# State attention and hard-swish FFN on one core: two pairs of w_out and the second batch's tokens are staged in the output tiles, and the order of the opening is written anew

## The chip, the cores and the metric

The kernel runs on one core of one Trainium2 chip. The metric is the device time of one execution in microseconds (us). A run of a kernel gives one such time; three runs of the kernel before gave 656.95, 657.22 and 658.18 us, median 657.22. A further execution was recorded by the hardware profiler; all times of single instructions come from it. The engines are TensorE (PE, with its weight loads shown apart as PEld), VectorE (DVE), ScalarE (ACT), GpSimd (POOL) and SyncE (SP), whose queue (SPq) issues almost all transfers. Each engine works through its own queue in order.

## The reference

Attention between tokens `x` (8 batches, 8 heads, 512 tokens, 64 columns) and a small state (32 rows per head), in both directions, and then a feed-forward layer over all 4352 result rows:

```python
scores  = scale * x @ state.T            # per batch and head: 512 x 32
a       = softmax(scores)                # over the 32 state rows
xread   = a @ state                      # 512 x 64
scores2 = scale * state @ x.T            # 32 x 512
sread   = softmax(scores2) @ x           # 32 x 64
y = concat([xread, sread], axis=2)       # 544 rows per batch, 8 heads x 64 = 512 columns
h = y @ w_in                             # 512 -> 2048
out = (h * clip(h + 3, 0, 6) / 6) @ w_out  # 2048 -> 512
```

Inputs and output are float32. (The reference draws `x` and the weights at random; 512 of the 544 rows of each batch are tokens, 32 are state rows.)

## The kernel before

**Work on PE.** The tokens' result is never formed: since `xread @ w_in` is `a @ (state @ w_in)`, the kernel forms, for each batch, W' = state x w_in ("wp", by `wprime`, matmuls at line 507) and then h = a x W' (`first`, line 977 for the first step of the first batch and 948 elsewhere). A *step* is one block of 128 columns of h: there are 16 per batch and 16 more for all batches' state rows. `first(n)` forms the block into a PSUM bank `ps_h`; ACT and DVE make g of it (lines 998 and 1000: a relu of h + 3 and then min and product) and split g into a high and a low part (`split`, lines 305 and 306, `g_hi` and `g_lo`); `second(n)` multiplies these with 128 rows of w_out into four accumulators `acc0` to `acc3`, three matmuls of 512 columns each (high x high, high x low, low x high). Step 0 of the first batch is done plainly, in full float32 (line 977 for its first product, 1017 for its second).

**Weights.** Each w_in and w_out piece is loaded in 16-bit halves by SP (`weight`, line 370) into a staging tile, and put together by ACT (line 379, into one of two `tops` tiles) and DVE (line 384, the "join"). w_in pieces are joined into their home `w_in0` to `w_in3`. w_out pieces are joined in place and then split into `w_out_hi` (ACT, line 410) and `w_out_lo` (DVE, line 412). Staging tiles are three `raw` tiles (512 KB each) and four `early` tiles, which are the later homes of w_out's last chunks; the table `PLACES` says which piece lies in which. A piece can only be loaded once the tile's earlier content has been used up.

**Attention.** For each batch the tokens are turned (`take_in`): the first batch on PE (line 617), later ones by transfers in blocks of 32 x 32 (`load_turned`, line 494, sixteen transfers into two `raw` tiles) and four stream transposes on DVE (line 607). Then come the scores by columns (`scores_by_columns`, line 507 with `tmp` and `stT`, or 520 for the first batch), the softmax on DVE and ACT, and the exponentials for the other direction, which are turned by a transpose on DVE into blocks (line 871, in a `raw` tile) and sixteen transfers (`weights_moved`, line 879, into another `raw` tile). The first batch's weights of the softmax are made in an output tile `ot` (key `bt`) by `tokens_by_rows`, turned by PE (line 713), and copied back (lines 715 and 716).

**Output tiles.** The pool `outp` has two tiles of 1 MB, tag `ot`. They hold the first batch's softmax, every third W' from the second batch on, and the finished rows of a batch before they are stored (line 1052).

**What sets the order.** The whole program is a plan: `T`, `V`, `S_` and `Q` add an operation of PE, DVE, ACT and SP's queue with an estimated cost, a rank, what it reads and writes and the buffers it takes; `Plan.order` puts all operations in one row, and each engine's queue is that row's operations of its engine. The table `OPENING` fixes the beginning of the row by operation numbers (631 of them); from there the planner takes, on each engine, the ready operation of the lowest rank by its estimated times. `issue` writes the instructions in that order, and up to the first product puts filler matmuls (`wake`) where the planner thinks that PE would stand idle.

Of the kernel before, what the change touches and what calls it, by code (L numbers as in the profile page):

```python
# [10 lines left out]
F32 = mybir.dt.float32  # L11
# [55 lines left out]
class Plan:  # L67
# [33 lines left out]
    def order(self):  # L101
# [22 lines left out]
        while len(row) < n_ops:  # L124
# [44 lines left out]
            if size:  # L169
                channel = max(channel, t + 0.5) + size / self.transfer  # L170
                done = max(channel, t) + 2.0
                flying.remove(min(flying))
                flying.append(done)
# [33 lines left out]
def tile_state_attention_then_hardswish_ffn(  # L207
# [8 lines left out]
    nc = tc.nc  # L216
# [73 lines left out]
    def Q(rank, size, do, reads=(), writes=(), after=()):  # L290
        return plan.add("Q", 0.49, rank, do, reads, writes, after, size)
# [974 lines left out]
```

## Time and profile before

| | |
|---|---|
| median of three runs | 657.22 us (656.95 to 658.18) |
| profiled execution | 655.46 us |
| its span, first to last instruction | 653.7 us |
| granted clock of PE, mean | 0.999 |
| PE busy | 641.6 us, 3934 matmuls |
| DVE busy | 393.0 us |
| ACT busy | 293.1 us |
| transfers | 46.25 MB in 135270 packets |

How to read the views: a *window* row gives the busy time of each engine in a stretch, the granted clock of PE, the busy share of the 16 DMA engines and what they moved. A *timeline* row gives start, duration, engine, line, operation, the tile written and the tiles read (numbers left out), partitions x elements, count, and in brackets how long the engine stood idle before it and what it waited for. The matmuls are pipelined: one that shows 0.39 us lies half over the next, so the distance of two starts says what one costs. A wait inside a group that was begun shows as a longer matmul, not as idle time. The *chain of waits* is the work that ended last, followed back from the end. SPq rows are the queue's own time for issuing; a row that covers several transfers includes the waits between them.

### The profile page before, as it was taken

The page shows a single profiled execution, that of the slowest core. Times are in us where ns is not written, and L with a number is a line of the kernel's source. Part 1 is how long each engine was busy: PE and PEld are TensorE (multiplying, and loading weights), DVE is VectorE, ACT ScalarE, POOL GpSimd, SP SyncE. Part 2 cuts the span into 40 slices and gives each one's busy share as a digit, 9 for nine tenths or more (in the row PEclk, how much of TensorE's full clock was granted, in tenths as well). Part 3 has the DMA queues.
Part 4 walks back from the last instruction along what each step waited for, and adds up shares of the span by engine and source line. Part 5 has one row for each costly group of instructions (what it writes and reads, how often), then busy time and mean ns, then how long its engine had stood idle before and what let it go on. Part 6 is the DMA issues. An engine that isn't in the chain of part 4 may idle for free.

```text
span 653.7 us, 9891 instructions
## 1 busy us (share of the span) xinstructions
PE 641.6 (98%) x3934; PEld 500.3 (77%) x3934; DVE 393.0 (60%) x685; ACT 293.1 (45%) x510; POOL 1.2 (0%) x7
## 2 busy tenths in 40 slices
PE   8999999989999999999999999999999999999997
PEld 6577778767877877787868777787778787788896
DVE  6988785468487356944686356834595344443552
ACT  5988454334344343633344344534344333433542
POOL 0000000000000000000000000000000000000000
PEclk9999999999999999999999999999999999999999
DMA  8985500604840503132131405041131001000101
GB/s 285 339 268 179 117 10 10 118 15 107 120 133 11 86 2 103 33 51 46 64 70 20 78 1 134 1 76 21 66 66 30 3 1 66 0 1 2 64 1 33
DMA packets 135270, 46.25 MB, mean 71 GB/s; under 512 B 123576, under 2 KB 129208, under 8 KB 135096
## 3 DMA queue, kind: packets, MB, share of 16 engines
q1 hardware_dynamic: 135080, 45.36, 28.5%
q8 instruction: 31, 0.51, 0.3%
q10 hardware_dynamic: 144, 0.26, 0.1%
q14 instruction: 15, 0.12, 0.1%
HBM read 33.02 MB, written 8.91 MB: 64 GB/s over the span
## 4 chain that ended last, share of the span: by engine, by line
PE 85%; SPq 4%; DMA 4%; DVE 3%; ACT 2%; issue 1%; DVEq 0%; ACTq 0%
PE acc L948 51%; PE ps_h L948 27%; PE ps_s L507 4%; PE ps_h L507 2%; SPq L879 1%; SPq L494 1%; DMA raw<-in_x_dram 1%; DMA early<-in_moe_w_out_dram 1%; PE ps_h L905 1%; SPq L478 1%; ACT tops L379 1%; DMA early<-in_moe_w_in_dram 1%; DMA raw<-raw 1%; DVE w_in L384 0%; ACT g L998 0%
## 5 line engine op out<-in xcount | busy, mean ns | idle before, releaser
L948 PE MATMUL acc<-w_out_hi,g_hi 128*128 128x512 f32 x540 | 213.4, 395 | 0.1
L948 PE MATMUL acc<-w_out_lo,g_hi 128*128 128x512 f32 x540 | 210.6, 390 | 0.0
L948 PE MATMUL acc<-w_out_hi,g_lo 128*128 128x512 f32 x540 | 210.2, 389 | 0.0
L998 ACT ACTIVATE g<-ps_h,three 128x512 f32<-128x512 f32 (+1 forms) x144 | 95.6, 664 | 221.9 <-PE ps_h L948 210.9
L1000 DVE SCALAR_TENSOR_TENSOR g<-g,ps_h 128x512 f32<-128x512 f32 (+1 forms) x144 | 94.3, 657 | 150.7 <-ACT g L998 149.9
L948 PEld LDWEIGHTS acc<-w_out_hi,g_hi 128*128 128x128 f32 x540 | 101.4, 188 | 34.5 <-issue 12.6
L306 DVE TENSOR_TENSOR g_lo<-g,g_hi 128x512 fp32r<-128x512 f32 (+1 forms) x143 | 93.9, 657 | 49.2 <-ACT g_hi L305 48.0
L305 ACT CAST g_hi<-g 128x512 fp32r<-128x512 f32 (+1 forms) x143 | 85.0, 595 | 85.1 <-DVE g L1000 80.3
L948 PEld LDWEIGHTS acc<-w_out_hi,g_lo 128*128 128x128 f32 x540 | 101.4, 188 | 21.7 <-DVE g_lo L306 0.2
L948 PEld LDWEIGHTS acc<-w_out_lo,g_hi 128*128 128x128 f32 x540 | 101.5, 188 | 19.6
L948 PE MATMUL ps_h<-aT_hi,wp_hi 128*128 128x512 f32 (+1 forms) x246 | 90.4, 367 | 3.3 <-DVE wp_lo L306 2.9
L948 PE MATMUL ps_h<-aT_hi,wp_lo 128*128 128x512 f32 (+1 forms) x246 | 89.1, 362 | 0.4 <-DVE wp_lo L306 0.4
L948 PE MATMUL ps_h<-aT_lo,wp_hi 128*128 128x512 f32 (+1 forms) x246 | 89.1, 362 | 0.0
L948 PEld LDWEIGHTS ps_h<-aT_hi,wp_hi 128*128 128x128 f32 x246 | 46.4, 189 | 13.4 <-issue 3.6
L948 PEld LDWEIGHTS ps_h<-aT_lo,wp_hi 128*128 128x128 f32 x246 | 46.4, 189 | 8.2 <-DVE aT_lo L306 0.5
L948 PEld LDWEIGHTS ps_h<-aT_hi,wp_lo 128*128 128x128 f32 x246 | 46.4, 189 | 7.8 <-DVE wp_lo L306 0.7
L948 PE MATMUL ps_h<-aT_hi,wp 128*128 128x512 f32 x144 | 50.2, 389 | 0.0
L948 PEld LDWEIGHTS ps_h<-aT_hi,wp 128*128 128x128 f32 x144 | 27.0, 188 | 5.7
L607 DVE STREAM_TRANSPOSE tmp<-raw 128x512 f32<-128x512 f32 x28 | 19.1, 699 | 15.9 <-DMA raw<-in_x_dram 12.3
L948 PE MATMUL ps_h<-aT_lo,wp 128*128 128x512 f32 x72 | 28.0, 389 | 0.0
L379 ACT CAST tops<-early 128x512 f16<-128x512 bf16 x25 | 18.2, 779 | 5.0 <-DMA early<-in_moe_w_out_dram 2.8
L507 PE MATMUL ps_s<-w_in,stT 64*32 64x512 f32 (+1 forms) x320 | 19.6, 548 | 0.0
(124 smaller groups left out, 427.4 us busy)
## 6 DMA issues: line engine op xcount, KB each, us to landing
xb<-in_x_dram SPq DMA_DIRECT2D x32, 256.0 KB, 4.2
out_dram<-ot SPq DMA_DIRECT2D x8, 1024.0 KB, 4.4
raw<-in_x_dram SPq DMA_DIRECT2D x112, 64.0 KB, 2.1
early<-in_moe_w_in_dram SPq DMA_DIRECT2D x7, 1023.0 KB, 5.8
early<-in_moe_w_out_dram SPq DMA_DIRECT2D x4, 1023.5 KB, 5.4
raw<-raw SPq DMA_DIRECT2D x112, 32.0 KB, 2.0
raw<-in_moe_w_out_dram SPq DMA_DIRECT2D x7, 511.8 KB, 7.1
early<-in_moe_w_in_dram SPq DMA_DIRECT2D x2, 511.0 KB, 6.4
```

Of the source, the lines that this page charges most:

```text
L305: S_(cost, rank, lambda: nc.scalar.copy(hi(), src()), reads, [writes[0]])
L306: V(cost, rank, lambda: nc.vector.tensor_tensor(lo(), src(), hi().bitcast(F32), op=ALU.subtract), [*reads, writes[0]], [writes[1]])
L379: nc.scalar.copy(out[..., 1], digits(pieces().bitcast(BF16), 2, i))
L478: nc.sync.dma_start(x_tile(b)[:, :, k, :], x_v[b, k])
L494: nc.sync.dma_start(t[rows, i].rearrange("t (a c) -> t a c", c=NS), x[b, 4 * g + 2 * i + u, :, k * NS : (k + 1) * NS].rearrange("(a t) c - ...
L507: nc.tensor.matmul(out[u][cols, :], made["stT", b][rows, cols], moving(q)[rows], start=True, stop=True,)
L607: V(0.7, rank[0], lambda q=q, key=key: nc.vector.transpose(xT(b, q), made[key][:, q % 2]), [(*key, q % 2, u, k) for u in range(2) for k in ...
L879: nc.sync.dma_start(dst[:, :, q], src[:, :, c])
L905: nc.tensor.matmul(bank(pr)[cols, u * D : (u + 1) * D], e2T(b, u)[:, j * P + q * NS : j * P + (q + 1) * NS], x_tile(b)[:, NG * q + u, j, : ...
L948: nc.tensor.matmul(ps, l, r, start=start and k == 0, stop=stop and k == n - 1)
L998: S_(cost + 0.05, rank, lambda: nc.scalar.activation(g(), bank(ps)[:, :width], AF.Relu, bias=three), [ps], [g_key])
L1000: V(cost, rank, lambda: nc.vector.scalar_tensor_tensor(g(), g(), 6.0, bank(ps)[:, :width], op0=ALU.min, op1=ALU.mult), [ps], [g_key])
```

## The change

Three things change.

1. In `PLACES`, the w_out pairs 4-5 and 6-7 no longer go to `early2` and `early3` but to output tiles (`("ot", ("w", 0))` and `("ot", ("w", 1))`, named `wide`), and their loads wait for the subtractions of the first softmax (`first_exps`). `early2` and `early3` so first hold w_in pair 8 and pair 10 (and w_out 3 before that in `early3`).
2. The second batch's turned tokens (`load_turned` and `take_in` for b = 1) go to an output tile instead of two `raw` tiles; for later batches they stay in `raw`.
3. `OPENING` is written anew, 670 numbers, and the planner's estimates of costs and of transfers are altered (a queue operation 0.53 for 0.49, 0.62 for a turned-token load, 0.65 for a move; the transfer's landing is counted from its share of the channel). These estimates enter the program only through the order.

```diff
 OPENING = """
-5 2 1 0 24 3 4 35 11 80 36 27 6 29 30 28 93 31 32 33 14 49 34 41 25 19 50 51 37 26 52 42 38 39 53 43 57 54 44
+5 0 1 2 11 3 4 33 24 80 34 27 93 28 31 29 6 30 32 35 19 41 36 12 14 49 42 43 160 37 13 44 39 38 45 50 40 46
...
             if size:
-                channel = max(channel, t + 0.5) + size / self.transfer
-                done = max(channel, t) + 2.0
+                channel = max(channel, t + 1.3) + size / self.transfer
+                done = channel + 1.6
...
+            if place[0] == "ot":
+                return get(place, lambda: outp.tile([P, 2, 512, 2], U32, name="wide", tag="ot"))
...
-        Q(load_rank, {("in", 1): 537.0, ("in", 2): 925.0, ("out", 1): 465.0, ("out", 2): 930.0}[kind, n], load, writes=[key])
+        Q(load_rank, {("in", 1): 537.0, ("in", 2): 960.0, ("out", 1): 465.0, ("out", 2): 1000.0}[kind, n], load, writes=[key],
+          after=first_exps if place[0] == 'ot' else ())
...
+    def turned_tile(key):
+        if key[0] == "raw":
+            return get(key, lambda: stage.tile([P, 2, S], F32, name="raw"))
+        return get(key, lambda: outp.tile([P, J, DO], F32, name="ot"))[:, 2 * key[2] : 2 * key[2] + 2]
...
-            key = ("raw", ("x", b, g))
+            key = ("raw", ("x", b, g)) if b > 1 else ("ot", ("x", b), g)
...
-                            t = get(key, lambda: stage.tile([P, 2, S], F32, name="raw"))
+                            t = turned_tile(key)
...
-                key = ("raw", ("x", b, q // 2))
+                key = ("raw", ("x", b, q // 2)) if b > 1 else ("ot", ("x", b), q // 2)
                 V(0.7, rank[0], lambda q=q, key=key: nc.vector.transpose(
-                    xT(b, q), made[key][:, q % 2]),
+                    xT(b, q), turned_tile(key)[:, q % 2]),
...
-            V(0.35, r[1], lambda m1=m1, view=view, bt=bt: nc.vector.tensor_tensor(
+            shifted = V(0.35, r[1], lambda m1=m1, view=view, bt=bt: nc.vector.tensor_tensor(
                 bt(), view(), wide(m1()), op=ALU.subtract), [m1_key, ps], [part_key])
+            first_exps.append(shifted)
...
-        ("in", 4): ("early0", 1), ("in", 6): ("early1", 1), ("out", 4): ("early2", 1),
-        ("out", 6): ("early3", 1), ("in", 8): ("early2", 2), ("in", 10): ("early3", 2),
+        ("in", 4): ("early0", 1), ("in", 6): ("early1", 1), ("out", 4): ("ot", ("w", 0)),
+        ("out", 6): ("ot", ("w", 1)), ("in", 8): ("early2", 2), ("in", 10): ("early3", 2),
```

What this does to the queues is seen in three places. Lines of the changed kernel are 3 to 11 higher.

**DVE at the end of the opening.** The rows run from the end of the first softmax to the g of step 0 (1000, now 1011). `w_in_314` and `w_in_308` hold the softmax's turned weights, `nm` the maxima for the other direction, `wp_lo` and `aT_lo` the low parts of W' and of the weights, and rows that end in `tops` are joins. Before:

```order
L781 TENSOR_REDUCE nm_297<-ps_s 128x2
L384 SCALAR_TENSOR_TENSOR w_in_179<-early_142,tops 128x4x128 x2
L716 COPY w_in_314<-acc_308 128x512
L781 TENSOR_REDUCE nm_297<-ps_s 128x2
L306 TENSOR_TENSOR wp_lo<-acc_253,wp_hi 128x128
L784 TENSOR_TENSOR nm_297<-nm_297 128x2
L306 TENSOR_TENSOR aT_lo<-w_in_314,aT_hi 128x512
L787 TENSOR_SCALAR nm_297<-nm_297 128x2
L306 TENSOR_TENSOR aT_lo<-w_in_314,aT_hi 128x512
L306 TENSOR_TENSOR wp_lo<-acc_252,wp_hi 128x128
L384 SCALAR_TENSOR_TENSOR early_168<-early_168,tops 128x512
L1000 SCALAR_TENSOR_TENSOR g<-g,ps_h 128x512
```

and of the change:

```order
L716 TENSOR_TENSOR ot<-ot,s_190 128x8x32 x2
L387 SCALAR_TENSOR_TENSOR w_in_216<-early_137,tops 128x4x128 x2
L307 TENSOR_TENSOR wp_lo<-acc_264,wp_hi 128x128
L727 COPY w_in_308<-acc_302 128x512
L307 TENSOR_TENSOR wp_lo<-acc_265,wp_hi 128x128
L387 SCALAR_TENSOR_TENSOR raw<-raw,tops 128x512
L307 TENSOR_TENSOR aT_lo<-w_in_308,aT_hi 128x512 x2
L792 TENSOR_REDUCE nm_337<-ps_s 128x2 x2
L1011 SCALAR_TENSOR_TENSOR g<-g,ps_h 128x512
L795 TENSOR_TENSOR nm_337<-nm_337 128x2
L798 TENSOR_SCALAR nm_337<-nm_337 128x2
L416 TENSOR_TENSOR w_out_lo_362<-raw,w_out_hi_214 128x512
```

The maxima `nm` have moved from between the joins and copies to a place behind `aT_lo`, and the join of w_out piece 3 (`early_168`, now `early_155`) has moved from before the g of step 0 to behind it.

**SP after the first weights.** The rows begin with the w_out pair 4-5, in `early_444` or `wide`; w_in pairs 4-5 and 6-7 stand ahead of them in both. `wide` are the two w_out pairs, `ot<-in_x_dram` and `raw<-in_x_dram` the turned tokens, `st_raw` the next batch's state. Before:

```order
L370 DMA early_444<-in_moe_w_out_dram 128x2x2047
L370 DMA raw<-in_moe_w_out_dram 128x2047
L370 DMA early_497<-in_moe_w_out_dram 128x2x2047
L440 DMA st_raw<-in_state_dram 32x4x32 x4
L370 DMA raw<-in_moe_w_out_dram 128x2047
L370 DMA early_562<-in_moe_w_in_dram 128x4x1023
L370 DMA early_595<-in_moe_w_in_dram 128x4x1023
L370 DMA early_641<-in_moe_w_out_dram 128x2x2047
L370 DMA early_683<-in_moe_w_out_dram 128x2x2047
L494 DMA raw<-in_x_dram 32x16x32 x16
```

and of the change:

```order
L373 DMA wide<-in_moe_w_out_dram 128x2x2047
L445 DMA st_raw<-in_state_dram 32x4x32 x4
L373 DMA wide<-in_moe_w_out_dram 128x2x2047
L373 DMA early_461<-in_moe_w_in_dram 128x4x1023
L373 DMA early_475<-in_moe_w_in_dram 128x4x1023
L373 DMA raw<-in_moe_w_out_dram 128x2047 x2
L504 DMA ot<-in_x_dram 32x16x32 x6
L373 DMA early_599<-in_moe_w_out_dram 128x2x2047
L504 DMA ot<-in_x_dram 32x16x32
L373 DMA early_612<-in_moe_w_in_dram 128x4x1023
L504 DMA ot<-in_x_dram 32x16x32
```

The two w_out pairs stand directly behind w_in pair 6-7 now (before, two w_in pairs and a single piece lay between), and the turned tokens of the second batch are spread around the pair of w_out 8-9 (`early_599`) and the last pair of w_in (`early_612`) instead of standing behind all pairs.

**DVE at the third batch's tokens.** The rows are the stream transposes of the third batch (607, now 617) with what stands around them. Before:

```order
L1000 SCALAR_TENSOR_TENSOR g<-g,ps_h 128x512
L306 TENSOR_TENSOR g_lo<-g,g_hi 128x512
L607 STREAM_TRANSPOSE tmp<-raw 128x512 x2
L306 TENSOR_TENSOR g_lo<-g,g_hi 128x512
L306 TENSOR_TENSOR wp_lo<-ps_s,wp_hi 128x512
L306 TENSOR_TENSOR wp_lo<-ps_h,wp_hi 128x512
L1000 SCALAR_TENSOR_TENSOR g<-g,ps_h 128x512
L306 TENSOR_TENSOR g_lo<-g,g_hi 128x512
L306 TENSOR_TENSOR wp_lo<-ps_s,wp_hi 128x512
L1000 SCALAR_TENSOR_TENSOR g<-g,ps_h 128x512
L607 STREAM_TRANSPOSE tmp<-raw 128x512 x2
L306 TENSOR_TENSOR wp_lo<-ps_h,wp_hi 128x512
```

and of the change:

```order
L456 STREAM_TRANSPOSE stT<-st_raw 128x128
L1011 SCALAR_TENSOR_TENSOR g<-g,ps_h 128x512
L307 TENSOR_TENSOR wp_lo<-ps_h,wp_hi 128x512
L617 STREAM_TRANSPOSE tmp<-raw 128x512
L307 TENSOR_TENSOR wp_lo<-ps_s,wp_hi 128x512
L307 TENSOR_TENSOR wp_lo<-ps_h,wp_hi 128x512
L307 TENSOR_TENSOR g_lo<-g,g_hi 128x512 x2
L307 TENSOR_TENSOR wp_lo<-ps_s,wp_hi 128x512
L617 STREAM_TRANSPOSE tmp<-raw 128x512
L1011 SCALAR_TENSOR_TENSOR g<-g,ps_h 128x512
L824 RECIPROCAL r_831<-r_831 128x2
L617 STREAM_TRANSPOSE tmp<-raw 128x512 x2
```

Before, all four `wp_lo` stood behind the first two transposes and the last of them behind all four; now the first stands ahead of all transposes, the other three between the first and the second, and the last two transposes have no `wp_lo` behind them.

More of the change, by code (lines that the diff above doesn't have):

```diff
@@ L288, in S_, with Q @@
         return plan.add("S", cost, rank, do, reads, writes, after)
-    def Q(rank, size, do, reads=(), writes=(), after=()):
-        return plan.add("Q", 0.49, rank, do, reads, writes, after, size)
+    def Q(rank, size, do, reads=(), writes=(), after=(), cost=0.53):
+        return plan.add("Q", cost, rank, do, reads, writes, after, size)
     def get(key, make):
@@ L392, in weight @@
             top = ("top", (kind, k + i))
-            S_(0.62, rank, lambda i=i: upper(i), [key], [top])
+            S_(0.65, rank, lambda i=i: upper(i), [key], [top])
             V(0.62, rank, lambda i=i: join(i), [key, top],
@@ L425, in tile_state_attention_then_hardswish_ffn @@
     wp_at, scores_at = {}, {}
+    first_exps = []
     def load_state(b, rank, after=()):
@@ L443, in load_state @@
         if b < TURNED:
-            plan.add("Q", 1.35, rank, load, (), [key], after, 400.0)
+            plan.add("Q", 1.39, rank, load, (), [key], after, 400.0)
             return
-        plan.add("Q", 1.8, rank, load_blocks, (), [key], after, 400.0)
+        plan.add("Q", 2.6, rank, load_blocks, (), [key], after, 400.0)
     def turn_state(b, rank, after):
@@ L499, in load @@
                             )
-                        Q(rank, 65.536, load, writes=[(*key, i, u, k)], after=after)
+                        Q(rank, 65.536, load, writes=[(*key, i, u, k)], after=after, cost=0.62)
     def all_heads(b, out, moving):
@@ L795, in exps @@
                                              accum_out=r2()[:, NG + NG * i + u : NG + NG * i + u + 1])
-                    S_(0.6, rank(5), exps, [ps[i], n_key], [("tmp", ("e2", b, u), i), (*r_key, u, i)])
+                    S_(0.48, rank(5), exps, [ps[i], n_key], [("tmp", ("e2", b, u), i), (*r_key, u, i)])
             V(0.08, rank(6), lambda: nc.vector.scalar_tensor_tensor(
@@ L865, in move @@
                             nc.sync.dma_start(dst[:, :, q], src[:, :, c])
-                        Q(rank, 16.384, move, [blocks_key], [e2T_key(b, g, c, q)])
+                        Q(rank, 16.384, move, [blocks_key], [e2T_key(b, g, c, q)], cost=0.65)
             return
@@ L879, in move @@
                     nc.sync.dma_start(dst[:, :, q], src[:, :, c])
-                Q(rank, 32.768, move, [(*blocks_key, g) for g in range(NG)], [e2T_key(b, 0, c, q)])
+                Q(rank, 32.768, move, [(*blocks_key, g) for g in range(NG)], [e2T_key(b, 0, c, q)], cost=0.65)
     def put(c, ps, cols):
```

45 rows, old and new, of the table OPENING are left out of this document.

## The prediction

> **What bounds the kernel now.** I read the page first, then the waits of PE, then the windows, then PE's timeline where a window showed a gap.
>
> ```profile
> span 653.7 us, 9891 instructions
> PE 641.6 (98%) x3934; PEld 500.3 (77%) x3934; DVE 393.0 (60%) x685; ACT 293.1 (45%) x510; POOL 1.2 (0%) x7
> PE 85%; SPq 4%; DMA 4%; DVE 3%; ACT 2%; issue 1%; DVEq 0%; ACTq 0%
> ```
>
> PE is busy for 98% of the span, so an edit can only win where PE idles, fills or waits inside an instruction. The windows say where that is:
>
> ```profile
> 10.00:20.00 10.00, 8.80 (x119) 6.57 (x119) 9.93 (x31) 8.99 (x19) 0.00 (x0) 1.00 1.04 390
> 20.00:30.00 10.00, 9.63 (x56) 4.26 (x54) 9.85 (x22) 9.41 (x23) 0.00 (x0) 1.00 0.94 324
> 40.00:50.00 10.00, 9.60 (x59) 7.08 (x58) 8.37 (x13) 9.01 (x16) 0.00 (x0) 1.00 0.77 238
> 130.00:140.00 10.00, 7.08 (x103) 4.80 (x101) 4.65 (x8) 2.62 (x4) 0.00 (x0) 1.00 0.19 32
> 200.00:250.00 50.00, 50.00 (x245) 40.05 (x245) 26.95 (x43) 19.96 (x33) 0.00 (x0) 1.00 0.20 32
> ```
>
> The columns are the window, its length, then PE, PEld, DVE and ACT busy. From 10 to 30 us DVE works 19.8 of 20 us: the opening is DVE's. At 130 to 140 PE loses 2.9 us with DVE half idle. After 200 us nothing is lost, and there the order of the work is the same in both kernels. So all that can change lies in the first 140 us:
>
> ```profile
> 23.57 2.07 PE L1017 MATMUL acc<-raw,g 128*128 128x512 f32 x4
> ...
> 44.03 0.39 PE L948 MATMUL acc<-w_out_hi,g_lo 128*128 128x512 f32 x1
> 44.82 0.50 PE L948 MATMUL ps_h<-aT_hi,wp_hi 128*128 128x512 f32 x1 [0.40 <-DVE g L1000]
> ...
> 54.52 0.40 PE L948 MATMUL ps_h<-aT_hi,wp_lo 128*128 128x512 f32 x1
> 54.95 0.51 PE L948 MATMUL ps_h<-aT_hi,wp_hi 128*128 128x512 f32 x1
> ...
> 76.16 2.12 PE L507 MATMUL ps_s<-tmp,stT 64*32 64x512 f32 x16
> ...
> 132.13 0.39 PE L948 MATMUL acc<-w_out_lo,g_hi 128*128 128x512 f32 x1
> 132.35 0.39 PE L948 MATMUL acc<-w_out_hi,g_lo 128*128 128x512 f32 x1
> 135.66 0.47 PE L948 MATMUL ps_h<-aT_hi,wp_hi 128*128 128x512 f32 x1 [2.92 <-DVE wp_lo L306]
> ...
> 138.01 1.09 PE L507 MATMUL ps_s<-tmp,stT 64*32 64x512 f32 x16
> ```
>
> Two 512-wide matmuls start 0.2275 us apart on average (132.13 and 132.35 are two); read the others against that. 44.03 to 44.82 is 0.56 too long, 54.52 to 54.95 is 0.20 too long. The scores of the second batch take 2.12 us at 76.16, the same sixteen of the third 1.09 at 138.01: 1.03 us of waiting that the profile books as busy. Then the plain gap of 2.92. Together 4.71 us.
>
> **The change part by part.** Both kernels have 687 instructions on DVE, 495 on ACT and 318 on SP in the order; PE has seven fillers, each a weight load and a matmul, fewer, 36 for 43. No work is removed: it is a matter of what stands before what.
>
> *Opening.* What ends it is the g of step 0, which releases the first product with w_out at 23.57:
>
> ```profile
> 22.83 0.68 DVE L1000 SCALAR_TENSOR_TENSOR g<-g,ps_h 128x512 f32<-128x512 f32 x1
> 23.43 0.68 DVE L384 SCALAR_TENSOR_TENSOR raw<-raw,tops 128x512 uint32<-128x512 uint32 x1
> 24.03 1.28 DVE L412 TENSOR_TENSOR w_out_lo<-raw,w_out_hi 128x512 fp32r<-128x512 f32 x2
> ...
> 32.22 0.74 DVE L306 TENSOR_TENSOR wp_lo<-ps_s,wp_hi 128x256 fp32r<-128x256 f32 x2
> ...
> 61.29 2.52 DVE L412 TENSOR_TENSOR w_out_lo<-early,w_out_hi 128x1024 fp32r<-128x1024 f32 x2
> ```
>
> A 512-wide operation costs DVE 0.60 us from start to start (22.83, 23.43, 24.03), a half-wide one 0.37, a double one 1.26. Ahead of this g stand seven joins of weights before and six now, and two operations on two columns fewer (about 0.07 each): 0.75 us less, if DVE stays full. It will not quite: the four reciprocals now follow each other with no join between them. I take 0.4 us; the ends are 1.2 (the cover holds and a second join slips behind) and −0.3 (the first piece of w_out that is now loaded ahead of w_in comes late). The product of step 0 now runs undivided, 4.1 us (two rows like that at 23.57), and covers the g_lo of step 1, which on DVE ends four operations of 0.60 and two small ones, about 2.6 us, behind the g.
>
> *The second pair of w_out.* The wait at 44.82 is on a g whose engine queue was held by this:
>
> ```profile
> 34.65 7.29 DMA early<-in_moe_w_out_dram
> 42.02 0.78 ACT tops L379
> 42.83 0.68 DVE early L384
> 43.51 0.57 issue
> 44.08 0.69 DVE g L1000
> ```
>
> This is the chain of waits, in order of time: the pair lands at 42.0, is joined, and only then comes the g. The pair goes to an output tile now; its tile is free once PE has turned the step-0 weights (18.7 us before), and a set of four small loads stands ahead on SP, so I put its issue at 22 and, with 7.3 us as in the first row, its landing near 30. The 0.56 goes, and with the queue looser the 0.20 at 54.95: 0.76 us.
>
> *Second batch's tokens.*
>
> ```profile
> 65.04 8.29 SPq L494 DMA_DIRECT2D raw<-in_x_dram  x16
> 73.44 0.42 SPq L370 DMA_DIRECT2D raw<-in_moe_w_out_dram  x1
> ...
> 76.45 0.71 DVE L607 STREAM_TRANSPOSE tmp<-raw 128x512 f32<-128x512 f32 x1 [1.55 <-DMA raw<-in_x_dram]
> ```
>
> The last of sixteen loads leaves at 73, and the fourth transpose of DVE waits for it until 76.45, inside the scores of 76.16. In the changed order the loads wait for w_out_lo of the first wide pair. On DVE that ends 19 operations of 0.60, six of 0.37, one of 1.26 and two small ones behind the g of step 0 (near 23.1): 15.1 us, and with 1 for waits near 39. Sixteen loads and two pairs between them at 0.6 end near 50; the last transpose could be done near 54. PE reaches these scores with 57 512-wide matmuls and one set like that of 138.01 (1.02 to the next row) fewer ahead of it: 57 x 0.2275 + 1.02 = 14.0 us, and 1.2 us of the gains above, so near 61. Seven us to spare; the 1.03 goes. A wait is added on SP: behind these loads stand two w_in and w_out pairs. The first is needed by ACT's queue near 48; it leaves near 43, and the row at 34.65 says 7.3 us for such a pair in traffic: up to 2 us late for ACT, but PE needs g of that step only near 55.
>
> *Third batch's tokens.*
>
> ```profile
> 131.98 0.60 SPq L494 DMA_DIRECT2D raw<-in_x_dram  x1
> 134.23 0.71 DVE L607 STREAM_TRANSPOSE tmp<-raw 128x512 f32<-128x512 f32 x1 [0.61 <-DMA raw<-in_x_dram]
> 134.86 0.65 DVE L306 TENSOR_TENSOR wp_lo<-ps_h,wp_hi 128x512 fp32r<-128x512 f32 x1
> ...
> 146.72 4.50 SPq L879 DMA_DIRECT2D raw<-raw  x7
> ```
>
> DVE stands at two transposes until the last load of 131.98 has landed; the wp_lo that PE wants is behind them. The loads share SP with the sixteen moves of the second batch, 0.64 us each (seven in 4.50). In the new order the blocks of the second batch stand in front of the end of its softmax on DVE; by the same counting they are done near 82, the second raw buffer that the moves need is free near 86, and the third batch's loads can begin near 95, when the last piece of w_out has left its buffer, behind the g of step 16. From there 28 issues at 0.62 end near 113, landing 115. In PE's order the third scores stand 7.5 us of matmuls earlier; with the gains that is 138.0 − 7.5 − 5.1, near 125. The wp_lo that stand between the transposes are wanted near 127. The 2.92 goes, with 8 us to spare.
>
> *What is late next.* Moving the second batch forward packs DVE. Between its scores and step 16 it has 41 operations of 0.60, a double one of 1.26 and 0.7 of small ones, 26.6 us; PE has 114 matmuls of 0.2275 and three sets of 1.02 there, 29.0 us. Before it was 23 and 0.8 of small ones, 14.6 us, against 57 matmuls and two sets, 15.0, which just held. 2.4 us are to spare, of which waiting for PE's own g takes a part; I add 0.4 us, between 0 and 2.5.
>
> The sum: −0.4 −0.76 −1.03 −2.92 +0.4 = −4.7 us. The profiled execution took 655.46 (span 653.7 and 1.8 around it), so 650.8 there. The median of the runs, 657.22, is 1.8 above it; 652.5 for the median.
>
> A row that speaks against the change:
>
> ```profile
> 37.00:50.00 13.00, 12.60 (x72) 9.57 (x71) 10.13 (x16) 11.53 (x19) 0.00 (x0) 1.00 0.80 253
> 65.00:73.50 8.50, 8.50 (x39) 7.06 (x38) 7.07 (x14) 4.66 (x10) 0.00 (x0) 1.00 0.65 108
> ```
>
> The last columns are DMA share and GB/s. The token loads alone use 0.65 of the DMA engines for 8.5 us, 5.5 us in all, at 108 GB/s. Now they go into a stretch that is at 0.80 for 13 us: 10.4 + 5.5 is 15.9, so 2.9 us of transfers spill over. The sum holds that nobody on PE's path waits for those; a rival holds otherwise. The Trainium skill, page "DMA: Bandwidth & Descriptors", section "Specifications", has such loads below line rate: it asks for pieces of at least 512 B, and these are 128 B. The trace agrees in direction (108 GB/s at 0.65 against 390 at 1.04), and by that rule the sum would be 4.7 less what spills, 1.8 us.
>
> **The rivals.**
>
> *DVE becomes the bound of steps 9 to 16.* For it: 26.6 of 29.0 us, a queue in order, a softmax that passes to ACT and back. Against: it held at 14.6 of 15.0. If every operation slips 10%, DVE needs 29.3, and with 2 us of waiting for PE's own g in that stretch 2.3 land on PE: −4.7 + 2.3, 654.8.
>
> *The transfers spill onto PE.* The late pair blocks ACT's queue, and with it g: −4.7 + 2.9, 655.4. Against: PE needs that pair's product only near 65.
>
> *The change does not do it:* the third batch's loads still need raw buffers that hold w_out, so DVE waits again ahead of wp_lo, and 2.92 stays: 655.4; with no gain in the opening either, 655.8. Against: 8 us to spare.
>
> *Slower.* The second batch's loads wait for an output tile; SP serves in order, so if that tile is freed late, the w_out pair of steps 8 and 9 is late too. It is wanted near 65; six loads at 0.6, 7.3 us of transfer and 4 us of joins and halves lie between, so it decides once the release comes after 50 instead of 39, and from then each us is one on PE. Release at 57 costs 7: 659.5. Against: at 39 DVE would have to lose 18 us.
>
> **How the numbers follow.** The forecast, 652.5, has 0.57 (from 650.9, the opening at 1.2 and no new wait, to 653.6). DVE late 0.18 (654.8), the spill 0.07 (655.4), the wait that stays 0.09 (655.4 to 656.5), slower 0.09 (658.6 and up). 0.2% is 1.3 us, about what a measurement of this kernel can tell from no change. Faster gets the forecast, DVE late, the spill and a small part of the third, 0.83; same 0.08; slower 0.09. For 8 in 10 the range runs from 650.9 to 655.8, less 0.2 and with the scatter of the median: 650.7 to 655.8.
>
> **What would show it.** Right: the first row of the w_out product near 23.2; no idle at the g of 44 us; the sixteen score matmuls of the second batch, near 61, in 1.1 us; no PE gap above 1 us between 100 and 140; the stream transposes of the second batch fed from the output tile and not waiting for a DMA. DVE near 95% from 60 to 90 with PE waiting for g_lo, aT_lo or wp_lo would be the first rival; ACT waiting for a w_out or w_in transfer at 45 to 55 us with PE idle behind it the second; a gap ahead of wp_lo with a transpose before it the third; SP standing at the token loads past 50 us the last. I am wrong altogether if PE loses time in a place that the old kernel had none.

## The result, and the profile after

| | us, median | lowest to highest | runs |
|---|---|---|---|
| before | 657.64 | 656.05 to 658.50 | 6 |
| changed | 650.88 | 650.19 to 651.82 | 6 |

The ratio is 0.990 (95%: 0.9885 to 0.9915): 6.8 us, 1.0% faster. The prediction was 652.5 in 650.7 to 655.8, so the median lies 0.2 us inside the lower end. The profiled execution took 651.16 us (span 649.2); against the profiled execution of before, 655.46, it is 4.3 us less, where the sum of the prediction had 4.7. One execution of e8 below, in a slow state with a granted clock of 0.82, took 736.57 us and is left out of e8's median.

The head of the page and its chain of waits (engines and their shares of the span):

```profile
span 649.2 us, 9880 instructions
PE 639.1 (98%) x3927; PEld 500.2 (77%) x3927; DVE 392.7 (60%) x685; ACT 293.5 (45%) x510; POOL 1.2 (0%) x7
PE 92%; DVE 3%; SPq 2%; DMA 1%; ACT 1%; issue 1%; DVEq 0%
```

The windows that were read of before, and three more (window, length, busy PE, PEld, DVE, ACT, POOL, granted clock, DMA share, GB/s):

```profile
10.00:20.00 10.00, 8.92 (x112) 6.43 (x113) 9.97 (x32) 8.94 (x19) 0.00 (x0) 1.00 1.04 393
20.00:30.00 10.00, 9.06 (x57) 4.55 (x57) 9.46 (x19) 9.44 (x23) 0.00 (x0) 1.00 1.06 375
40.00:50.00 10.00, 10.00 (x71) 7.10 (x70) 9.62 (x19) 9.13 (x17) 0.00 (x0) 1.00 0.96 244
50.00:60.00 10.00, 9.35 (x42) 7.41 (x40) 5.39 (x10) 5.90 (x10) 0.00 (x0) 1.00 0.74 189
60.00:70.00 10.00, 8.98 (x117) 5.46 (x117) 9.75 (x19) 5.38 (x10) 0.00 (x0) 1.00 0.33 106
70.00:80.00 10.00, 10.00 (x50) 7.99 (x43) 10.00 (x16) 7.29 (x12) 0.00 (x0) 1.00 0.00 0
130.00:140.00 10.00, 10.00 (x46) 8.28 (x45) 6.86 (x15) 4.93 (x10) 0.00 (x0) 1.00 0.00 0
200.00:250.00 50.00, 50.00 (x245) 40.09 (x244) 24.88 (x39) 18.80 (x30) 0.00 (x0) 1.00 0.25 51
```

From 40 to 50 and from 130 to 140 PE is now full. From 70 to 80 DVE is busy for 10.00 of 10.00 and PE too: the packed DVE costs nothing. But from 50 to 70 PE loses 1.7 us where it lost next to nothing before. The rows of PE there, and of the opening and the third batch's scores (start, duration, what, and the idle ahead with its releaser):

```profile
21.86 3.42 PE L1028 MATMUL acc<-raw,g 128*128 128x512 f32 x7 [0.94 <-DVE g L1011]
...
58.97 0.39 PE L959 MATMUL acc<-w_out_hi,g_lo 128*128 128x512 f32 x1
60.37 1.05 PE L517 MATMUL ps_s<-tmp,stT 64*32 64x512 f32 x4 [1.02 <-DVE tmp L617]
62.07 1.08 PE L517 MATMUL ps_s<-tmp,stT 64*32 64x512 f32 x12 [0.66 <-DVE tmp L617]
63.08 1.10 PE L916 MATMUL ps_h<-xb,tmp 128*32 128x64 f32 x64
...
126.38 0.27 PE L934 MATMUL ps_h<-ident,tmp 128*128 128x128 f32 x1
126.58 1.09 PE L517 MATMUL ps_s<-tmp,stT 64*32 64x512 f32 x16
```

The scores of the second batch end at 63.08 and could have begun at 59.19 (58.97 and one step of 0.2275): 3.89 us for what takes 1.11 where nothing waits. Before, the same stretch took 2.14 (the scores start at 76.16 there, the next row at 78.21). What DVE waited for, and what SP did (SP's rows are the issues of transfers):

```profile
58.92 1.30 DVE L617 STREAM_TRANSPOSE tmp<-ot 128x512 f32<-128x512 f32 x2 [4.36 <-DMA ot<-in_x_dram]
```

```profile
39.40 4.93 SPq L504 DMA_DIRECT2D ot<-in_x_dram  x6
44.44 0.42 SPq L373 DMA_DIRECT2D early<-in_moe_w_out_dram  x1
44.91 0.47 SPq L504 DMA_DIRECT2D ot<-in_x_dram  x1
45.47 0.44 SPq L373 DMA_DIRECT2D early<-in_moe_w_in_dram  x1
45.95 0.65 SPq L504 DMA_DIRECT2D ot<-in_x_dram  x1
46.70 0.47 SPq L373 DMA_DIRECT2D raw<-in_moe_w_out_dram  x1
47.22 11.05 SPq L504 DMA_DIRECT2D ot<-in_x_dram  x8
```

The first load leaves at 39.4, as forecast. The last eight, without a wait on any engine, take 11.05 us to be issued, in place of some 4 at the 0.49 that most issues take.

### The profile page after: what moved, and what is told of

Its sections match the earlier page's. It is cut to its first block, busy times and chain, and to the rows that moved or that the text cites. A ratio compares the mean times of both kernels' runs of the same rounds, so it can differ in the third digit from the quotient of the medians.

```text
span 649.2 us, 9880 instructions
## 1 busy us (share of the span) xinstructions
PE 639.1 (98%) x3927; PEld 500.2 (77%) x3927; DVE 392.7 (60%) x685; ACT 293.5 (45%) x510; POOL 1.2 (0%) x7
## 4 chain that ended last, share of the span: by engine, by line
PE 92%; DVE 3%; SPq 2%; DMA 1%; ACT 1%; issue 1%; DVEq 0%
PE acc L959 55%; PE ps_h L959 29%; PE ps_s L517 4%; PE ps_h L517 2%; SPq L504 2%; PE ps_h L916 1%; DMA raw<-in_moe_w_out_dram 1%; DVE w_in L387 1%; PE acc L1028 1%; DMA ot<-in_x_dram 0%; ACT tops L382 0%; DVE g L1011 0%; SPq L438 0%; DVE raw L387 0%; DVE ot L716 0%
## 5 line engine op out<-in xcount | busy, mean ns | idle before, releaser
L307 DVE TENSOR_TENSOR wp_lo<-ps_h,wp_hi 128x512 fp32r<-128x512 f32 x18 | 11.8, 687 | 16.4 <-ACT wp_hi L306 16.4
L307 DVE TENSOR_TENSOR wp_lo<-ps_s,wp_hi 128x512 fp32r<-128x512 f32 (+1 forms) x32 | 18.2, 599 | 0.4 <-ACT wp_hi L306 0.2
```

Source lines behind the costliest of these rows:

```text
L307: V(cost, rank, lambda: nc.vector.tensor_tensor(lo(), src(), hi().bitcast(F32), op=ALU.subtract), [*reads, writes[0]], [writes[1]])
```

## The experiments

Each kernel ran in turn with the kernel before; ratios are to that, with 95% intervals.

| kernel | us, median | ratio |
|---|---|---|
| e1 tokens first | 650.17 | 0.9910 (0.9886 to 0.9933) |
| e2 two halves behind | 649.68 | 0.9901 (0.9879 to 0.9923) |
| e3 long pieces | 649.39 | 0.9893 (0.9873 to 0.9913) |
| e4 old opening | 652.78 | 0.9943 (0.9925 to 0.9960) |
| e5 changed again | 650.63 | 0.9908 (0.9892 to 0.9923) |
| e7 pairs only | 661.08 | 1.0061 (1.0044 to 1.0078) |
| e8 as e2 | 649.07 | 0.9890 (0.9872 to 0.9909) |
| e9 late turns (on before) | 652.80 | 0.9943 (0.9921 to 0.9965) |
| e10 two moves (on before) | 654.70 | 0.9974 (0.9958 to 0.9990) |
| e11 join back | 651.72 | 0.9935 (0.9912 to 0.9958) |

e6 and e12 are the kernel of before again, one execution each: 658.14 and 656.59. Groups of them ran on different chips. By the ratios, e1 to e3 do not differ from the changed kernel (0.990, and 0.9908 in e5): what they show, they show in their traces.

**The new wait at 60 us: e1, e2, e3.** Three theories: the loads leave late because small pieces among weights hold up SP (A); they start too late (B); the bytes are too many (C).

e1, SP's order (and the decodes of these weights moved down on ACT and DVE):

```diff
-L373 DMA raw<-in_moe_w_out_dram x2
-L504 DMA ot<-in_x_dram x6
-L373 DMA early<-in_moe_w_out_dram
-L504 DMA ot<-in_x_dram
-L373 DMA early<-in_moe_w_in_dram
-L504 DMA ot<-in_x_dram
-L373 DMA raw<-in_moe_w_out_dram
-L504 DMA ot<-in_x_dram x8
+L504 DMA ot<-in_x_dram x16
+L373 DMA early<-in_moe_w_out_dram
+L373 DMA early<-in_moe_w_in_dram
+L373 DMA raw<-in_moe_w_out_dram x3
```

> The changed kernel with the sixteen loads of the second batch's tokens issued one after the other, and the three loads that stood among them, and two of w_out that stood ahead, behind them; the decodes of those weights stand a few rows later on ACT and DVE. Theory A (the loads leave late because SP stands at issues of 1.3 to 2.6 us among the weights, 0.49 us each otherwise): the last token load leaves before 50 us in place of 57.8, the 4.36 us idle of DVE ahead of the stream transposes is under 0.5, PE's two waits there (1.02 and 0.66) go, and the sixteen scores with their waits take 1.1 to 1.4 us in place of 3.9: 2.5 to 2.9 us off, about 648.2 where the changed kernel has 650.9. Theory B (they start too late, at 39.4, when the tile comes free, and the order behind does not matter): the transposes still wait, 650.5 to 651. Theory C (it is the amount of bytes, and whoever comes last waits): the w_out pair of steps 8 and 9 is now late instead, ACT waits for it and g behind it, 650.5 to 652.

SP's issues in e1:

```profile
40.21 8.30 SPq L504 DMA_DIRECT2D ot<-in_x_dram  x16
48.63 1.91 SPq L373 DMA_DIRECT2D early<-in_moe_w_out_dram  x1
```

All sixteen leave in 8.30 us, 0.52 each, the last before 48.6; DVE no longer waits for them and the scores cost 1.11. That is A's side of the expectation, but the time fell only to 650.17. PE's rows show why:

```profile
67.15 1.04 PE L517 MATMUL ps_s<-w_in,stT 64*32 64x512 f32 x2
68.41 1.09 PE L517 MATMUL ps_s<-w_in,stT 64*32 64x512 f32 x14 [0.21 <-DVE tmp L766]
```

These sixteen run until 69.4 and take 2.3 us where such a set takes 1.1: some 1.1 us came back. PE waited for DVE's transposes out of that bank; the reduction ahead of them ran at 63.95 (63.07 in e2), behind joins that my order had moved down. C was right in kind (whoever is moved behind is late), though not in who.

e2 moves only two half loads of w_out, neither wanted before 60 us:

```diff
-L373 DMA raw<-in_moe_w_out_dram x2
+L373 DMA raw<-in_moe_w_out_dram
...
-L504 DMA ot<-in_x_dram
-L373 DMA raw<-in_moe_w_out_dram
-L504 DMA ot<-in_x_dram x8
+L504 DMA ot<-in_x_dram x9
+L373 DMA raw<-in_moe_w_out_dram x2
```

> The changed kernel with only two half loads of w_out moved behind the sixteen token loads: one that stood just ahead of them, one among them. Theory A: one place fewer where SP stands, and 0.5 MB less ahead; the last token load leaves near 54 to 55 and 1 to 2 us of the 2.9 go: about 649.4. Theory B: no change, 650.9. Theory C: 1.0 MB at 390 GB/s is 2.6 us of transfers less in front, the wait shrinks to nearly nothing, about 648.4.

PE in e2:

```profile
60.28 0.39 PE L959 MATMUL acc<-w_out_hi,g_lo 128*128 128x512 f32 x1
60.59 1.09 PE L517 MATMUL ps_s<-tmp,stT 64*32 64x512 f32 x16
61.61 1.10 PE L916 MATMUL ps_h<-xb,tmp 128*32 128x64 f32 x64
```

The wait is wholly gone (A expected about half of it to go, C nearly all, so here C was nearer), and nothing comes back: in e2 every window from 30 to 200 us has PE full. The last token load leaves near 54.7: that was early enough, it need not be 50.

e3 keeps the order and reads the same bytes of the second batch's tokens in longer pieces:

```diff
+if b == 1:
+    nc.sync.dma_start(
+        t[rows, i],
+        x[b, 4 * g + 2 * i + u].rearrange("(t a) c -> t (a c)", a=S // D)[k * NS : (k + 1) * NS],
+    )
+    return
```

> The changed kernel in its own order; each of the sixteen loads of the second batch's tokens reads the same 64 KB in pieces of 2 KB in place of 128 B, which puts the tokens of that batch in another order (the values of the second batch are not the reference's). Theory A (many small pieces fill the queue, so that SP stands at the issue): the issues take 0.5 us throughout, the last leaves near 50, the wait goes: about 648.3. Theory C (bytes alone): the bytes are the same, so the last load leaves after 55 and the time stays within 0.5 of 650.9. Theory B: also no change.

The windows of 40 to 62 us, of the changed kernel and then of e3:

```profile
40.00:62.00 22.00, 20.40 (x115) 14.68 (x113) 17.01 (x32) 15.79 (x26) 0.00 (x0) 1.00 0.77 197
```

```profile
40.00:62.00 22.00, 22.00 (x190) 16.26 (x192) 20.21 (x37) 17.48 (x30) 0.00 (x0) 1.00 0.65 210
```

PE is full, and the DMA engines are busy for 0.65 x 22 = 14.3 us in place of 16.9 at a slightly higher rate. So the length of the pieces is a cause by itself: C as bytes alone, which expected no change, falls. Whether the pieces act through the issues on SP or through the time of the DMA engines, e3 does not separate, since it shortens both. A's detail was off: the last load still left at 54.5, since SP now waited for earlier transfers instead of standing inside an issue. B falls with all three: they start at 40.2 to 40.7, later than the changed kernel's 39.4, and don't wait.

**How much of it is usual: e5, e8.** The changed kernel and e2, each once more and side by side.

> The changed kernel once more. In its first profile the first product with w_out starts at 21.86; three kernels with the same opening had it at 22.68, 23.17 and 22.73. If the opening varies with the landing of the first loads and the tokens' landing does not follow it (the wait ahead of the second batch's scores takes the difference up), the span stays within 0.7 of 649.2 though the opening ends near 22.8, and the scores with their waits cost 2.5 to 3.2 us in place of 3.9. If the opening's delay passes on, the span is near 650.1 and the scores cost 3.9 again.

> The changed kernel with the two half loads of w_out behind the token loads, once more and with more rounds, beside the changed kernel. The wait of 3.9 us less 1.1 was gone in its profile while its median was only 1.2 below the changed kernel's of another call. If the whole wait is worth its size in a usual execution, 2.5 to 2.8 us below the changed kernel; if part of that wait only took up what the opening varies by, 1.0 to 1.8 below.

In e5 the first product starts at 22.15 and the second batch's scores are one row:

```profile
59.26 0.39 PE L959 MATMUL acc<-w_out_hi,g_lo 128*128 128x512 f32 x1
59.58 2.27 PE L517 MATMUL ps_s<-tmp,stT 64*32 64x512 f32 x16
61.77 1.10 PE L916 MATMUL ps_h<-xb,tmp 128*32 128x64 f32 x64
```

2.29 us with its waits, 1.2 too long, where the first profile had 2.8 too long; its span is 647.9. So the size of this wait varies between executions; neither branch of the expectation fits, since the opening was hardly later. With the two halves behind, the medians are 1.2 and 1.6 us below the changed kernel's (649.68 and 649.07 against 650.88 and 650.63), about what e5's wait is worth. But only e8 and e5 ran side by side, and the intervals of their ratios overlap; the ratios of the other pair, 0.9901 and 0.990, show no difference. So e2's trace shows the wait gone; that this version is faster than the changed kernel is likely and not shown.

**The kernel of before again: e6, e12.**

> The kernel of before once more, for its profile: the first was taken of an execution of 655.46, under all six timed runs (656.05 to 658.5). If the time that the others have on top lies in the gap ahead of the third batch's scores (2.92 in the first profile), that gap is now 4 to 5 us; if it lies in the opening, the first product with w_out starts 1 to 2 us later than 23.57 and the gap is the same.

> The kernel of before a third time, for its profile. Its timed runs lie between 654.4 and 658.7. If what separates them is the clock behind the gap ahead of the third batch (half for 3.41 us in the execution of 658.14, not in that of 655.46): an execution above 657 shows that drop again, about 1.9 us, and one below 656 doesn't. If it is something else (the opening, the tokens of the second batch): an execution above 657 with the clock at 1.0 throughout.

PE in e6, at the gap ahead of the third batch:

```profile
132.97 0.39 PE L948 MATMUL acc<-w_out_hi,g_lo 128*128 128x512 f32 x1
136.61 0.77 PE L948 MATMUL ps_h<-aT_hi,wp_hi 128*128 128x512 f32 x1 [3.25 <-DVE wp_lo L306]
137.18 0.63 PE L948 MATMUL ps_h<-aT_lo,wp_hi 128*128 128x512 f32 x1
137.60 0.63 PE L948 MATMUL ps_h<-aT_hi,wp_lo 128*128 128x512 f32 x1
```

```profile
136.00:138.00 2.00, 1.39 (x3) 1.16 (x4) 1.66 (x3) 0.31 (x1) 0.00 (x0) 0.63 0.00 0
138.00:140.00 2.00, 2.00 (x6) 1.58 (x5) 0.00 (x0) 0.42 (x2) 0.00 (x0) 0.52 0.00 0
```

After 3.25 us of idling the matmuls start 0.42 apart in place of 0.2275: the granted clock is 0.63 and 0.52 in two windows of 2 us, and 1.00 in those around. Up to the row before the gap e6 stands 0.6 us behind the first profile, behind it 2.5: 0.3 is the longer gap, 1.5 the clock. The first profile (2.92 idle) and e12 (2.66) kept 1.00. The Trainium skill, page "TensorE: Matmul & The Clock Gate", section "Part 1: The HAM clock gate", says that an idle window of some 3.4 us halves PE's clock, and that the windows run freely. The trace agrees in direction, with a drop after 3.25 and none after 2.92 and 2.66, though 3.25 is below that figure; these few waits do not tell what their length does from what their place in the windows does. e12 took 656.59, between the two bounds set for it, without a drop: the clock is not all that separates the executions of before.

The granted clock of each timed run is on record, as a mean over the execution, and tells more. Of the 17 runs of before beside e9 to e11, nine have 0.999 or 1.0 and took 654.4 to 657.1 us (median 655.4); eight have 0.995 or 0.997, as e6 has 0.997, and took 656.7 to 658.7 (median 657.9). Of the 33 runs of before beside e1 to e11, 19 have 0.997 or less; of the ten of the changed kernel none is under 0.998. So more than half of the executions of before lost clock, and the first profile is of one that did not. The mean does not say where in an execution the clock was lost, and the gap cannot be the only place: one run each of e1, e2 and e8 and two of e11 have 0.993 to 0.995. The profiles side by side:

| | first | e6 | e12 | changed | e5 |
|---|---|---|---|---|---|
| first product with w_out starts | 23.57 | 23.49 | 23.50 | 21.86 | 22.15 |
| wait for g at 44 us | 0.4 | 0.8 | 0.9 | 0 | 0 |
| second batch's scores with waits | 2.14 | 2.43 | 2.72 | 3.89 | 2.29 |
| idle ahead of the third batch | 2.9 | 3.3 | 2.7 | 0 | 0 |
| lost to the clock behind it | 0 | 1.5 | 0 | 0 | 0 |
| span | 653.7 | 656.4 | 654.8 | 649.2 | 647.9 |

The first profile of before has the smallest waits of the three at 44 us and at the second batch's scores, and no loss of clock.

**The third batch's gap: e9, e7.** e9 is the kernel of before with one move on DVE:

```diff
-L607 STREAM_TRANSPOSE tmp<-raw 128x512 x2
 L306 TENSOR_TENSOR wp_lo<-ps_h,wp_hi 128x512
 L306 TENSOR_TENSOR g_lo<-g,g_hi 128x512
 L1000 SCALAR_TENSOR_TENSOR g<-g,ps_h 128x512
+L607 STREAM_TRANSPOSE tmp<-raw 128x512 x2
```

> The kernel of before with one change on DVE: the two stream transposes of the third batch that wait for its tokens stand three rows later, behind the wp_lo, g_lo and g that PE waits for. If the gap ahead of the third batch is DVE's queue standing at the transposes (2.9 us, and 3.3 in the second profile, there with a granted clock of 0.5 for 3.41 us behind it): wp_lo runs near 130, the gap shrinks to under 1 us at the scores, the clock stays at 1.0, and 2 to 4.5 us go: 653 to 655 beside 657. If the gap belongs to the tokens themselves (the scores simply wait for them instead): 656.5 to 657.5, with the idle at the scores in place of ahead of wp_lo.

DVE in e9, and PE at the scores:

```profile
130.38 0.69 DVE L306 TENSOR_TENSOR wp_lo<-ps_h,wp_hi 128x512 fp32r<-128x512 f32 x1
131.15 0.69 DVE L306 TENSOR_TENSOR g_lo<-g,g_hi 128x512 fp32r<-128x512 f32 x1
133.18 0.69 DVE L1000 SCALAR_TENSOR_TENSOR g<-g,ps_h 128x512 f32<-128x512 f32 x1 [1.33 <-ACT g L998]
133.78 1.30 DVE L607 STREAM_TRANSPOSE tmp<-raw 128x512 f32<-128x512 f32 x2
```

```profile
134.92 0.27 PE L923 MATMUL ps_h<-ident,tmp 128*128 128x128 f32 x1
135.13 1.09 PE L507 MATMUL ps_s<-tmp,stT 64*32 64x512 f32 x16
```

wp_lo runs at 130.38, the transposes find their data and end as PE arrives; PE doesn't wait, and 3.9 us of the median go (652.80 beside 656.68; 2.3 to 5.2 by the interval). No run of e9 has a clock under 0.998, and beside the runs of before that kept theirs (655.4) it wins 2.6: the 3.9 is the gap and, in about half of the runs, lost clock; that this was lost behind the gap, as in e6, is likely. So the gap was the queue of DVE standing at two rows, not the tokens, and by the medians two moved rows are worth more than half of the change's 6.8.

e7 goes the other way: the changed order up to about 31 us and both pairs in output tiles, then the order of before with the tokens in staging buffers.

```diff
...
-key = ("raw", ("x", b, g)) if b > 1 else ("ot", ("x", b), g)
+key = ("raw", ("x", b, g))
...
-key = ("raw", ("x", b, q // 2)) if b > 1 else ("ot", ("x", b), q // 2)
+key = ("raw", ("x", b, q // 2))
```

> The changed order up to about 31 us with both pairs of w_out in output tiles; from there the order of before, and the second batch's tokens in the staging buffers as before. If the parts of the change add up: the opening's 1.7 and the 0.76 at the second pair of w_out are won, the scores of the second batch keep their 1 us of waiting and the gap of 2.9 ahead of the third batch's stays: 2 to 2.5 us under before, 654 to 655 where before has 656.5 to 657.6. If the opening's gain is taken up by the later waits: within 0.7 of before, 656 to 657. If the gap is not tied to where the second batch's tokens are staged but to the wide pairs, it is gone: 651 to 652.

```profile
PE ps_h L959 <- DVE wp_lo L307: 3.3, 1, 3.3
PE acc L959 <- ACT g_hi L306: 3.0, 1, 3.0
PE acc L959 <- DVE w_out_lo L416: 1.6, 1, 1.6
```

These are PE's waits in e7 (us in total, times, longest). The gap ahead of wp_lo stays, so opening and pairs don't remove it. The parts don't add up, though: e7 is 4.2 us slower than before, by two waits at 36 to 41 us (the second and third row) that neither kernel has; the granted clock is 0.83 over 30 to 50 us and, behind the gap, over 140 to 150. In the old order ACT decodes the w_in pair that is now loaded behind the two wide pairs before it does the g_hi that PE wants; it stood 4.46 us for that transfer. This comes of joining two orders; it says only that the wide pairs do not go with the order of before behind them.

**The wait at 44 us: e10.** As e9, and the g ahead of the joins:

```diff
+L1000 SCALAR_TENSOR_TENSOR g<-g,ps_h 128x512
 L384 SCALAR_TENSOR_TENSOR early<-early,tops 128x512 x2
-L1000 SCALAR_TENSOR_TENSOR g<-g,ps_h 128x512 x2
+L1000 SCALAR_TENSOR_TENSOR g<-g,ps_h 128x512
```

> The same, and the g that PE waits for at 44 us stands ahead of the two joins of the second pair of w_out in place of behind them. If that wait was the queue's and not the transfer's: no idle there, 0.5 to 0.8 us less than with the one move: 652.3 to 654.4. If the wait moves on to the next row that needs the pair: as with the one move.

DVE and then ACT in e10:

```profile
43.99 0.69 DVE L1000 SCALAR_TENSOR_TENSOR g<-g,ps_h 128x512 f32<-128x512 f32 x1 [2.57 <-ACT g L998]
44.60 1.29 DVE L384 SCALAR_TENSOR_TENSOR early<-early,tops 128x512 uint32<-128x512 uint32 x2
```

```profile
42.01 1.41 ACT L379 CAST tops<-early 128x512 f16<-128x512 bf16 x2 [1.26 <-DMA early<-in_moe_w_out_dram]
43.28 0.68 ACT L998 ACTIVATE g<-ps_h,three 128x512 f32<-128x512 f32 x1
```

Neither: 1.9 us worse than e9. The g runs no sooner, since it waits 2.57 us for ACT's half of it, and ACT's queue stands at the decode of the same pair until that has landed; the joins are only later. So DVE's queue alone is not the cause. Two explanations are left: the transfer, which the changed kernel starts at 22.4 in place of 34.7, and ACT's queue, which stands idle for 1.26 us ahead of the decode while the ps_h that its g needs was done near 39. Moving that g ahead of the decode on ACT was not tried.

**The opening: e4, e11.** e4 gives the list its first 106 entries from before:

```diff
 OPENING = """
-5 0 1 2 11 3 4 33 24 80 34 27 93 28 31 29 6
+5 2 1 0 24 3 4 35 11 80 36 27 6 29 30 28 93
```

> The changed kernel with the order of before, on all queues, up to and with the first g of step 0; from there its own order. In the traces that g starts at 21.13 (changed) and 22.83 (before). If the opening's 1.7 us reach the end: g near 22.8 again, the release of the first output tile near 41 in place of 39.3, the token loads that much later, and the time 1.4 to 1.8 above the changed kernel's: 652.3 to 652.7. If the wait for the tokens takes them up (the landing is set by the transfers and not by DVE): under 0.5 above, 651.3.

e11 puts one join of a w_out piece back ahead of the first g:

```diff
+L387 SCALAR_TENSOR_TENSOR early<-early,tops 128x512
 L1011 SCALAR_TENSOR_TENSOR g<-g,ps_h 128x512
...
-L387 SCALAR_TENSOR_TENSOR early<-early,tops 128x512
```

> The changed kernel with the join that went behind the g of step 0 put back ahead of it, as before. By the count of DVE's rows 0.60 us of the opening: the first product with w_out 0.6 later than the 21.9 to 23.2 of the profiles of the changed opening. If the wait ahead of the second batch's scores takes it up (2.29 and 3.89 in two profiles, 1.11 without a wait): 650.6 to 650.9, as the changed kernel. If it passes on: 651.2.

e11 costs 1.1 us against 650.63 (1.8 by the ratios), a little more than expected. In its trace PE stands idle for 1.58 us ahead of the first product, in place of 0.94 in the changed kernel: the 0.64 between them is the join. The product starts at 23.63, the second batch's scores are reached 37.1 us behind it as in the changed kernel, and with their waits they cost 2.93, between the 2.29 and 3.89 of that kernel. So the join's 0.6 passes on; the rest is within the scatter.

e4 costs 1.9 us against 650.88 (2.8 by the ratios), but it does not price the opening. Its first product starts at 22.82, no later than in e1 to e3, which ran beside it with the new opening (22.68, 23.17 and 22.73). Its scores are reached 38.8 us behind the product in place of 37.1: 1.7 us are lost between, most of it where PE waits 1.3 for a wp_lo at 30 to 35 us, at the place where the two orders are joined.

## Why the prediction was right, and where it was not

- **The sum held, and the step to the median did not.** It said 650.8 for the profiled execution (651.16 measured) and then added 1.8 because the median of before stood that far above its profile. The changed kernel's median is 0.3 under its profile. What lay between profile and median in before goes mostly with the clock: the runs that kept it have a median of 655.4, as the profile's 655.46, and those that lost some 657.9. Larger sizes of the very waits that the change removes add to it (the table of e6 and e12). No run of the changed kernel is under 0.998, so the offset didn't carry over.
- **Opening: right in kind, its size unsettled.** Forecast 0.4 with 1.2 as the end; the two first profiles differ by 1.71. One join less on DVE is 0.6 of it (e11). Another 0.53 is a wait of the first join on DVE (the row at 9.33 us of before), and that goes with neither order: with the old opening e4, e9 and e10 do not have it, and with the new one the first join of e2, e3 and e11 waits 0.24 to 0.39. The changed opening ended at 21.86, 22.15, 22.44, 22.68, 22.73 and 23.17 in six profiles (mean 22.5), that of before between 23.05 and 23.57 in five (mean 23.3), and at 22.82 in e4. About 0.8 is an estimate of its usual worth from these means; pairs that ran side by side differ by 1.3 (e6 and e5) and by nothing (e4 and e1 to e3).
- **Second pair of w_out: right in the result.** No wait at 44 us, PE full from 30 to 50. e10 shows that DVE's order was not the cause; between the transfer and ACT's queue it does not decide. The pair that I saw landing near 30 was issued at 22.4 as forecast and landed at 33.6, after 11.1 us in place of 7.3, and cost nothing.
- **Second batch's tokens: wrong.** "Seven us to spare; the 1.03 goes" failed at its first half: I counted sixteen loads at 0.6 us, ending near 50; the last left at 57.8, since five issues took 1.3 to 2.6. In place of −1.03 the term is +1.75 in the first pair of profiles, and between −0.4 and +0.2 with e5. The row against the change that I quoted (15.9 us of transfers in a stretch of 13) pointed at this stretch; e1 and e3 show that it takes the order of the issues and the short pieces too. I had its spill land on the late w_out pair; it landed on the tokens themselves, the last in SP's order.
- **Third batch's tokens: right, and worth more than its size.** Forecast 2.92; the first pair of profiles gives 3.1 from start to start. e9 shows that it was DVE's queue standing at the transposes, and worth 3.9 in the median. In the changed kernel two things have changed there: the tokens are loaded by 117 in place of 132, and a wp_lo stands ahead of the first transpose. Either could be enough; no run separates them. I put PE at those scores near 125; it was there at 126.6.
- **DVE packed: no cost.** 10.00 of 10.00 from 70 to 80 and PE as full. The 0.4 was not needed, and the rival that rested on it did not occur.
- **Not listed:** before, PE waited 0.3 to 0.5 us near 180 us for DVE to empty an accumulator bank into the first output tile; in the changed kernel that wait is gone.
- **Slower:** the output tile came free at 39.3, near the 39 counted, so the mechanism never came into play. Two errors met in that: g of step 0 ended at 21.8 in place of 23.1, and the release came 17.5 us behind it in place of 16.1.

So in the first pair of profiles the second batch's term was 2.8 us too hopeful, and the opening 1.3, DVE 0.4, the gap 0.2 and the unlisted wait 0.3 too cautious. These leave 0.6; the times differ by 0.4 from the sum (4.7 and 4.3), and the spans by 0.2, so the terms themselves hold to some 0.4. That the total came so near is luck: its largest error was hidden by the others.

What stays open: whether the wait at 44 us was the transfer's or ACT's queue's; what the opening is usually worth; what decides, beside a wait near 3 us, whether the clock is lost; and why SP stands at some issues for 2.5 us and not at others. e1 and e3 show that weights among the tokens and short pieces are both needed, not the mechanism.

## What to carry to other kernels

When a row in an in-order queue waits for a transfer, ask first which rows behind it could stand ahead: two moved rows gave 3.9 us here without touching a buffer. When loads of many short pieces move into a stretch of long ones, budget them by the share of the DMA engines that they used alone, and put last in the queue what is wanted last. And the offset between profile and median belonged to the waits of the kernel before and to the clock lost behind them: look at the granted clock of the timed runs before carrying such an offset over to a kernel without those waits.

## What the runs showed of the hardware

- An issue of the same 64 KB load took SP 0.49 us, and 1.3 to 2.6 us five times among weights; in pieces of 2 KB it took 0.31 to 0.50.
- A wait of PE of 3.25 us (e6) and one of 3.3 (e7) were followed by a clock of half for 3.41 us, and in e7 also one of 3.0, with a second wait one matmul behind it; waits of 2.66 and 2.92 were not. In e6 the lost clock cost 1.5 us.
- The same opening, with the same loads, varied by 1.3 us over six executions on more than one chip.
